# All five late token tiles summed by scaled and transposed rows, one tile after the other; gathered v rows turned by half blocks everywhere

## The chip, the cores and the metric

The kernel runs on one core of one Trainium2 chip. The metric is the device time of one execution in microseconds (us). Engines are named as the profile names them: PE (TensorE, the matrix unit), DVE (VectorE), ACT (ScalarE), POOL (GpSimd, here only the issuer of gathers) and SP (SyncE, the issuer of all other transfers).

## What is computed

2048 tokens of width 576 pass through two branches and a gate:

```python
g = sigmoid((x * gate_w).sum(-1, keepdims=True))
a = irfft2(rfft2(x) * (w_r + 1j * w_i))            # spectral branch
q = einsum("nd,dhc->nhc", x, w_q)                  # 32 heads, two halves of 128
s1, s2 = q[..., :128] @ k1.T, q[..., 128:] @ k2.T  # 64 scores each
i1, i2 = argmax(s1), argmax(s2)                    # one expert of 4096 per token and head
e = i1 * 64 + i2
gain = softmax(best s1 + best s2)                  # over one candidate
act = gelu(einsum("nd,nhd->nh", x, u[e]))
b = einsum("nh,nh,nhd->nd", gain, act, v[e])       # expert branch
out = g * a + (1 - g) * b
```

## The kernel before

**Tiles and chunks.** The tokens are 16 tiles of 128; the 32 heads are 8 chunks of 4. For each of the 64 pairs of (chunk, two tiles) PE multiplies x by a folded query matrix (`mh`, `ml`, x split into `xh`, `xo`, `xq`, so that products are exact enough for an argmax), DVE takes the maxima (L577), ACT and DVE turn them into expert numbers (L584 to L633). For each tile, chunk and head POOL then issues one indirect transfer (L671) that brings 128 rows of 4608 bytes, u and v of the chosen experts side by side, into a buffer `uv`. There are 512 such gathers. 12 buffers hold them, 15 from the second half on; the matrices for the next chunk (`uv<-wqT`) use the same 12.

**What is done with a gathered group of four rows** (function `group`): DVE takes the four dot products of u and x (L683), ACT the gelu (L689), DVE multiplies by the gain (L698; L693 in the very last group, head by head). Then the v rows are summed over the heads in one of two ways, which `how(t, c)` picks:
- "v": DVE multiplies each v row by its factor and adds it to an accumulator (L709 for the first, L711 for the others). The buffer is free after that.
- "t": ACT scales each v row (L724); scaled rows of two heads stand side by side in one buffer, and PE transposes this pair block by block into PSUM, where the heads are added. The buffers are free after that. An early tile adds each chunk's PSUM to `yt` on DVE (L771) and is turned back at the end (L1115); a late one stays in PSUM over its chunks and is turned back by PE at its end, with two ACT copies (L754, L758).

PE's transposes come in two forms (`turn`): whole blocks (9 matmuls of 128x128 for a pair), or half blocks, 64 rows each on half of the array (18 matmuls of 64 columns for a pair). `HALF` is for early tiles and `HALF_L` for late ones. `TJ` and `TJ_L` say after how many rows PE is called.

**Stages.** Tiles 0 to 10 are "early": their gathers run while PE works on the scores. Tiles 11 to 15 are "late": their gathers come after all early ones, in the order of `SEQ`, while PE, ACT and DVE work on the spectral branch: a first stage on x (`fold`; tiles in `FOLD_V` add and subtract the halves of x on DVE first, L889 and L891, and need fewer matmuls), the middle (`f2`, `f4`, `f5`, `f6`, L917 to L1057), and the inverse (`invert`; tiles not in `INV_P` do two DVE steps, L1094 and L1095, in place of half of the last matmuls). `mix` (L1115, L1118) puts both branches together, and SP writes the tile.

**The order** of each engine's instructions is written out ahead by a planner (`Plan.order`): it runs through the jobs with assumed durations, priorities (`at`) and pools, and each engine then works strictly in the order found. Numbers such as `LEAD`, `TPS`, `TLAG`, `XN0` or `BUILD` are its assumptions and priorities: they move instructions and change none. All engines' instructions of a kind come from one line (all PE work is L372), so the profile tells them apart by tiles.

The lines around which the change turns, before:

```python
if mode == "v":
    ...
        dv(0.731, at, lambda v=v, s=s: stt(y.ap, v(), s(), y.ap, op0=ALU.mult, op1=ALU.add), [y], [(rows[k], 1), (a, k)])
    return
last = c == NCH - 1 - (TAILV if t == SEQ[-2][0] and t in T_T else 0)
...
half = HALF_L if t >= NE else HALF
for k in range(HPC):
    if mode == "t":
        ...
        ac(0.667, at + AT_SCALE, ...)          # L724
        tj = TJ_L if t >= NE else TJ
        if k % tj < tj - 1:
            continue                           # PE is called after tj rows
```

Of the kernel before, what the change touches and what calls it, by code (L numbers as in the profile page):

```python
# [27 lines left out]
NCH = 8  # L28
# [60 lines left out]

LAG = {"DVE": 0.1, "ACT": 0.2, "PE": 0.0}  # L90
HOPS = {('PE', 'DVE'): 0.12, ('PE', 'ACT'): 0.46, ('PE', 'POOL'): 0.64, ('ACT', 'PE'): 0.28, ('ACT', 'DVE'): 0.02, ('ACT', 'POOL'): 0.01, ('DVE', 'POOL'): 0.4}
LEAD = 1.341
LEAST = -11.809
LAND = 4.039
ALONE = 0.716
SHARE = 0.426
WINDOW = 3.41
DENSE = -2.439
SLOWER = 1.649


class Plan:
# [37 lines left out]
    def order(self):  # L140
# [77 lines left out]
        while events:  # L218
            t = events[0][0]
            while events and events[0][0] <= t:  # L220
# [26 lines left out]
            for eng, q in todo.items():  # L247
# [60 lines left out]
def tile_kernel(ctx, tc, xn, xT, wqT, wqL, kT, wri, uv, uw, gw, t_kr, t_fi, t_fe, t_tw, t_io, out):  # L308
# [151 lines left out]
    last = {}  # L460
# [200 lines left out]
    def group(t, c, at, ahead, gate_by=()):  # L661
# [49 lines left out]
                    dv(0.731, at, lambda v=v, s=s: stt(y.ap, v(), s(), y.ap, op0=ALU.mult, op1=ALU.add), [y], [(rows[k], 1), (a, k)])  # L711
            return
        part = t in E_T
        last = c == NCH - 1 - (TAILV if t == SEQ[-2][0] and t in T_T else 0)
        part_ = part and not paired(t, c)
        first = c == 0 or (part and not paired(t, c - 1))
        if first:
# [459 lines left out]
TPS = 7.047
AHEAD = -45.811
TLAG = 27.448
FPACE = 1.413  # L1180
# [26 lines left out]
ISSUE = 0.845
MOVE = 1.368
X_GAP = 4.311
GATE = -10.202  # L1210
HOLD_ML = 1.992
HOLD_A = 0.08
HOLD_T = 0.263
# [5 lines left out]
AT_GELU = -46.223
AT_SCALE = 9.213  # L1220
AT_SUM = -94.03
AT_FOLD = -9.381
# [11 lines left out]
TP0 = 12.235
X2 = 59.927
X4 = -0.154
XN0 = 11.008
INV_P = (0, 1, 2, 4, 8, 9, 10, 12, 14, 15)
SOLO = 0
SOLO_AT = -7.687  # L1240
SGO0 = 22.859
SOLO_P = 222.219
GL0 = 208.398
GL = 1.201
# [66 lines left out]
```

## Time and profile before

| | |
|---|---|
| median of 3 runs | 948.02 us (943.16 to 948.95) |
| profiled execution, its own time | 941.52 us |
| its span, first to last instruction | 939.7 us, 18504 instructions |
| mean granted PE clock | 0.972 |
| busy: PE, DVE, ACT, POOL | 866.9, 815.9, 641.3, 559.1 us |
| transfers | 344.16 MB, of which 302.02 MB are gathers |

A row of the windows view gives, for a stretch of the span, the busy time of each engine with its number of instructions, the granted PE clock (1.00 is full), the mean busy share of the 16 DMA engines, and GB/s. Shares just over 1 come from packets that overlap. A row of the groups gives line, engine, operation, tiles, shapes and count, then the busy time in us and the mean duration of one in ns, then the engine's idle time just ahead of it and what ended that. A row of the timeline gives start, duration, engine, line and operation, and in brackets the idle time ahead and its releaser.

### The profile page before, as it was taken

Reading aid. Unit: us, or ns where it says so; the run is one execution under the profiler, and the core shown is the slowest. Engines: PE = TensorE matmul, PEld = TensorE weight load, DVE = VectorE, ACT = ScalarE, POOL = GpSimd, SP = SyncE. Lnnn points to the kernel's source line nnn. Section 1 sums busy time; section 2 is a strip of 40 time slices with the busy share of each in tenths; the row PEclk is TensorE's granted clock in tenths of the full one; section 3 lists DMA queues with packets and bytes.
Section 4 is the critical chain, followed back from the end, with each engine's and each line's share of the span. In section 5 each row is a group of like instructions: output and inputs, shape, how many; then the busy total and the mean of one; then the engine's idle time right before and its main releaser. Section 6 shows DMA issues by size and latency. Waiting matters only on the chain. (4 is left out here: it accounts for less than half of the span.)

```text
span 939.7 us, 18504 instructions
## 1 busy us (share of the span) xinstructions
PE 866.9 (92%) x6309; PEld 699.4 (74%) x6309; DVE 815.9 (87%) x2036; ACT 641.3 (68%) x2022; POOL 559.1 (59%) x516
## 2 busy tenths in 40 slices
PE   7899999999999998999999999967989999979993
PEld 6678887887877887888787777755767788756662
DVE  3578998998999999899999989898988898887888
ACT  3779888877877776876877777664646656654443
POOL 0416767756756656665665665667666556667560
PEclk9999999999999999999999999997999999999997
DMA  8968999999999999999999999899999999999993
GB/s 272 380 224 314 386 404 363 397 401 372 365 393 368 384 391 361 360 390 380 362 400 386 383 391 417 317 337 415 328 417 341 367 380 395 415 351 412 379 419 131
DMA packets 93218, 344.16 MB, mean 366 GB/s; under 512 B 10306, under 2 KB 14020, under 8 KB 93124
## 3 DMA queue, kind: packets, MB, share of 16 engines
q0 software_dynamic: 73728, 302.02, 83.7%
q1 hardware_dynamic: 19396, 40.96, 11.9%
q8 instruction: 50, 0.82, 0.3%
q14 instruction: 44, 0.36, 0.1%
HBM read 338.22 MB, written 4.72 MB: 365 GB/s over the span
## 5 line engine op out<-in xcount | busy, mean ns | idle before, releaser
L584 ACT ACTIVATE sg<-p,mx 128x64 bf16<-128x64 f32 x1024 | 227.1, 353 | 86.8 <-DVE mx L577 63.3
L671 POOL DMA_INDIRECT uv<-uv,eq x176 | 189.5, 1077 | 161.8 <-DVE xn L711 48.1
L683 DVE SCALAR_TENSOR_TENSOR uv<-uv,xn 128x576 f32<-128x576 f32 x352 | 259.9, 749 | 13.9 <-DMA uv<-uv,ei 4.6
L671 POOL DMA_INDIRECT uv<-uv,ei x178 | 199.9, 1123 | 104.8 <-issue 32.5
L724 ACT ACTIVATE uv<-uv,a 128x576 f32<-128x576 f32 x316 | 223.3, 784 | 19.7 <-DVE a L698 16.2
L372 PE MATMUL p<-ident,uv 64*128 64x64 f32 (+1 forms) x1980 | 159.7, 249 | 13.8 <-ACT uv L724 9.6
L372 PEld LDWEIGHTS p<-ident,uv 64*128 64x128 f32 (+1 forms) x1980 | 138.7, 140 | 41.3 <-ACT uv L724 16.7
L711 DVE SCALAR_TENSOR_TENSOR xn<-uv,a,xn 128x576 f32<-128x576 f32 x190 | 154.2, 812 | 0.5
L671 POOL DMA_INDIRECT uv<-uw,eq x80 | 88.2, 1103 | 52.5 <-issue 13.6
L683 DVE SCALAR_TENSOR_TENSOR uv<-uv,xl 128x576 f32<-128x576 f32 x160 | 116.0, 751 | 0.2
L372 PE MATMUL p<-mh,xha 128*128 128x512 f32 x256 | 106.3, 415 | 3.6 <-issue 2.4
L671 POOL DMA_INDIRECT uv<-uw,ei x78 | 81.2, 1042 | 41.0 <-issue 15.3
L372 PE MATMUL p<-mh,xh 128*128 128x512 f32 x256 | 103.5, 404 | 0.4 <-ACT sg L584 0.4
L372 PE MATMUL p<-ml,xha 128*128 128x512 f32 x256 | 101.1, 395 | 1.4 <-issue 1.4
L372 PE MATMUL p<-ml,xh 128*128 128x512 f32 x256 | 101.2, 395 | 0.6 <-issue 0.6
L372 PE MATMUL p<-mh,xoa 128*128 128x512 f32 x256 | 101.0, 395 | 0.5 <-issue 0.3
L372 PE MATMUL p<-mh,xo 128*128 128x512 f32 x256 | 101.1, 395 | 0.0
L372 PE MATMUL p<-fi,bt 128*128 128x289 f32 (+1 forms) x384 | 89.9, 429 | 1.1 <-ACT bt L917 0.7
L577 DVE TENSOR_REDUCE mx<-p 128x16 f32<-128x1024 f32 x64 | 77.9, 1218 | 13.9 <-PE p L372 11.8
L372 PEld LDWEIGHTS p<-fi,bt 128*128 128x128 f32 (+1 forms) x384 | 67.6, 242 | 19.1 <-issue 12.1
L606 ACT ACTIVATE sg<-sg 128x256 bf16<-128x256 bf16 x192 | 73.6, 424 | 0.8
L689 ACT ACTIVATE b<-z 128x4 f32<-128x4 f32 (+1 forms) x131 | 29.8, 228 | 62.7 <-DVE uv L683 52.1
(142 smaller groups left out, 1333.4 us busy)
## 6 DMA issues: line engine op xcount, KB each, us to landing
uv<-wqT SPq DMA_DIRECT2D x32, 512.0 KB
w<-wri SPq DMA_DIRECT2D x16, 289.0 KB
ml<-xT SPq DMA_DIRECT2D x16, 256.0 KB
xn<-xn SPq DMA_DIRECT2D x11, 288.0 KB
out<-xn SPq DMA_DIRECT2D x10, 288.0 KB
uv<-uv,ei POOLq DMA_INDIRECT x178
uv<-uv,eq POOLq DMA_INDIRECT x176
uv<-wqL SPq DMA_DIRECT2D x8, 256.0 KB
```

Source lines behind the costliest of these rows:

```text
L372: after("PE", nc.tensor.matmul(*args, **kw))
L577: dv(dve(1024), at - MXO, lambda: nc.vector.tensor_reduce(mv.ap[:, 2 * tp : 2 * tp + 2, :], ps.ap.rearrange("p a (g e) -> p a g e", e=E), ...
L584: on("ACT", actv(sg.ap[:, j, g, :], ps.ap[:, j, g * E : g * E + E], AF.Sign, bias=mv.ap[:, 2 * tp + j, g : g + 1], scale=-1.0))
L606: ac(0.307 if j is None else 0.2, at_, lambda b=b, s2=s2: actv(s2()[:, :, b * Q : b * Q + Q], s2()[:, :, b * Q : b * Q + Q], AF.Copy, bias ...
L671: on("POOL", nc.gpsimd.indirect_dma_start(out=g.ap.rearrange("p a d -> p (a d)"), out_offset=None, in_=table, in_offset=bass.IndirectOffse ...
L683: dv(0.677, at, lambda k=k, g=rows[k]: stt(g.ap[:, 0, :], g.ap[:, 0, :], 1.0, x.ap, op0=ALU.mult, op1=ALU.mult, accum_out=z.ap[:, k : k + 1]),
L689: ac(0.1, at + AT_GELU, lambda k0=k0, k1=k1: actv(b.ap[:, k0:k1], z.ap[:, k0:k1], AF.Gelu_apprx_tanh), [(b, k0)], [(z, k) for k in ks], ta ...
L711: dv(0.731, at, lambda v=v, s=s: stt(y.ap, v(), s(), y.ap, op0=ALU.mult, op1=ALU.add), [y], [(rows[k], 1), (a, k)])
L724: ac(0.667, at + AT_SCALE, lambda k=k, pair=pair, r=r: actv(pair.ap[:, r, :], rows[k].ap[:, 1, :], AF.Copy, scale=a.ap[:, k : k + 1]), [(p ...
```

## The change

- Late tiles. Before, tile 15 was summed the "v" way in all chunks, and tile 11 the "t" way except for its last chunk; the two were interleaved chunk by chunk at the end. Now all five late tiles are "t", one after the other (11, 14, 12, 13, 15), and only the last chunk of the last tile, 15, is "v". PE is called after two rows, not four (`TJ_L`).
- Early tiles. Six of eleven stay "t" (others than before), now with half blocks (`HALF`).
- Spectral branch. 3 tiles in place of 11 fold on DVE first; 7 in place of 10 do the long form of the inverse.
- The first pair of tiles is handled tile by tile (`SOLO`: two maxima of 512, L573, in place of one of 1024), and the planner's numbers differ, so that everything is in a new order.

```diff
-        last = c == NCH - 1 - (TAILV if t == SEQ[-2][0] and t in T_T else 0)
+        last = c == NCH - 1 - tail(t)
...
-LEAD = 1.341
+LEAD = 0.765
...
-BUILD = (3, 5, 6, 7, 7)
+BUILD = (2, 5, 5, 6, 6)
...
-_PAIRS = ((14,), (13,), (12,), (11, 15))
+_PAIRS = ((11,), (14,), (12,), (13,), (15,))
...
-HALF = 0
+HALF = 1
 HALF_L = 1
+TAILW = 1
...
-TJ_L = 4
+TJ_L = 2
...
-T_T = (2, 3, 4, 6, 7, 10, 11, 12, 13, 14)
+T_T = (1, 3, 5, 6, 7, 10, 11, 12, 13, 14, 15)
...
-FOLD_V = (0, 1, 4, 5, 6, 8, 10, 11, 12, 13, 14)
+FOLD_V = (0, 3, 8)
...
-TAILV = 1
+TAILV = 0
...
-INV_P = (0, 1, 2, 4, 8, 9, 10, 12, 14, 15)
-SOLO = 0
+INV_P = (0, 1, 4, 6, 7, 14, 15)
+SOLO = 1
...
+def tail(t):
+    if t not in T_T:
+        return 0
+    return TAILW if t == SEQ[-1][0] else TAILV if t == SEQ[-2][0] else 0
...
 def how(t, c):
-    if t == SEQ[-2][0] and c >= NCH - TAILV:
+    if c >= NCH - tail(t):
         return "v"
```

**Where instructions move.** First, the end of DVE's order. Of the two accumulators before, `xn_11043` is tile 11's and `xn_10218` tile 15's. Before:

```order
L683 SCALAR_TENSOR_TENSOR uv_10922,z_11050<-uv_10922,xl_7143 128x576
L711 SCALAR_TENSOR_TENSOR xn_11043<-uv_10877,a_11048,xn_11043 128x576
L693 SCALAR_TENSOR_TENSOR a_11061<-b_11053,gone,swl_7718 128x1 x2
L711 SCALAR_TENSOR_TENSOR xn_11043<-uv_10899,a_11048,xn_11043 128x576
L693 SCALAR_TENSOR_TENSOR a_11061<-b_11053,gone,swl_7718 128x1
L711 SCALAR_TENSOR_TENSOR xn_10218<-uv_10903,a_11061,xn_10218 128x576
L683 SCALAR_TENSOR_TENSOR uv_10960,z_11050<-uv_10960,xl_7143 128x576
L711 SCALAR_TENSOR_TENSOR xn_10218<-uv_10914,a_11061,xn_10218 128x576
L693 SCALAR_TENSOR_TENSOR a_11061<-b_11053,gone,swl_7718 128x1
L1118 SCALAR_TENSOR_TENSOR xn_11043<-xn_11043,gone,xl_10858 128x576
L711 SCALAR_TENSOR_TENSOR xn_10218<-uv_10922,a_11061,xn_10218 128x576
L711 SCALAR_TENSOR_TENSOR xn_10218<-uv_10960,a_11061,xn_10218 128x576
```

And now (`xn_12251` is tile 15's sum, turned back; `xn_10516` tile 13's):

```order
L683 SCALAR_TENSOR_TENSOR uv_11985,z_12174<-uv_11985,xl_7713 128x576
L693 SCALAR_TENSOR_TENSOR a_12187<-b_12184,gone,swl_8513 128x1 x2
L683 SCALAR_TENSOR_TENSOR uv_12011,z_12174<-uv_12011,xl_7713 128x576
L1118 SCALAR_TENSOR_TENSOR xn_10516<-xn_10516,gone,xl_12210 128x576
L693 SCALAR_TENSOR_TENSOR a_12187<-b_12184,gone,swl_8513 128x1
L683 SCALAR_TENSOR_TENSOR uv_12034,z_12174<-uv_12034,xl_7713 128x576
L693 SCALAR_TENSOR_TENSOR a_12187<-b_12184,gone,swl_8513 128x1
L1118 SCALAR_TENSOR_TENSOR xn_12251<-xn_12251,gone,xl_12214 128x576
L711 SCALAR_TENSOR_TENSOR xn_12251<-uv_11954,a_12187,xn_12251 128x576
L711 SCALAR_TENSOR_TENSOR xn_12251<-uv_11985,a_12187,xn_12251 128x576
L711 SCALAR_TENSOR_TENSOR xn_12251<-uv_12011,a_12187,xn_12251 128x576
L711 SCALAR_TENSOR_TENSOR xn_12251<-uv_12034,a_12187,xn_12251 128x576
```

Before, the sums of two tiles alternate at the end; now only the four of tile 15 are left, and they stand behind the mixing of what PE has turned back.

Second, the end of PE's order (`ident,uv` are transposes of gathered pairs, `fi,bt` and `t,krb` the inverse, `ident,f` the turning back). Before:

```order
L372 MATMUL p_1430_10927<-fi_7148,bt_7496 128x289 x6
L372 MATMUL p_1434_10949<-fi_7148,bt_7496 128x289 x6
L372 MATMUL p_1432_10970<-t_1431_10958,krb_7157 128x289 x4
L372 MATMUL p_1625_10180<-ident,uv_10694 128x64 x18
L372 MATMUL p_1625_10180<-ident,uv_10752 128x64 x18
L372 MATMUL p_1436_11021<-t_1435_10975,krb_7157 128x289 x4
L372 MATMUL p_1712_11032<-ident,f_1711_11027 128x128 x4
L372 MATMUL p_1712_11032<-ident,f_1711_11027 128x64 x2
```

And now:

```order
L372 MATMUL p_1419_12110<-fi_7717,bt_8170 128x289 x6
L372 MATMUL p_1670_11720<-ident,uv_11809 128x64 x18
L372 MATMUL p_1417_12146<-t_1416_12122,krb_7747 128x289 x4
L372 MATMUL p_1670_11720<-ident,uv_11856 128x64 x18
L372 MATMUL p_1421_12177<-t_1420_12144,krb_7747 128x289 x4
L372 MATMUL p_1670_11720<-ident,uv_11879 128x64 x18
L372 MATMUL p_1670_11720<-ident,uv_11945 128x64 x18
L372 MATMUL p_1714_12241<-ident,f_1713_12237 128x128 x4
L372 MATMUL p_1714_12241<-ident,f_1713_12237 128x64 x2
```

More transposes stand among the last matmuls of the inverse, and they come one pair at a time.

Third, the start of SP's order (`ml<-xT` is one tile of x for the scores, `mh<-xT` the remainder of four tiles, `xn<-xn` a tile of x for the dot products, `uv<-wqT` a query matrix). Before:

```order
L482 DMA xn_123<-xn 128x576
L482 DMA xn_125<-xn 128x576
L473 DMA ml_129<-xT 128x512
L473 DMA ml_135<-xT 128x512
L482 DMA xn_139<-xn 128x576
L482 DMA xn_150<-xn 128x576
L473 DMA ml_259<-xT 128x512
L469 DMA mh_266<-xT 128x4x128
```

And now:

```order
L473 DMA ml_123<-xT 128x512
L473 DMA ml_125<-xT 128x512
L482 DMA xn_129<-xn 128x576
L482 DMA xn_135<-xn 128x576
L482 DMA xn_139<-xn 128x576
L482 DMA xn_150<-xn 128x576
L428 DMA uv_159<-wqT 128x1024
L473 DMA ml_270<-xT 128x512
L469 DMA mh_274<-xT 128x4x128
```

Tiles 2 and 3 of x moved ahead of the xn rows, and a query matrix of the second chunk (`uv_159`) moved up ahead of the fifth tile.

More of the change, by code (lines that the diff above doesn't have):

```diff
@@ L91 @@
 HOPS = {('PE', 'DVE'): 0.12, ('PE', 'ACT'): 0.46, ('PE', 'POOL'): 0.64, ('ACT', 'PE'): 0.28, ('ACT', 'DVE'): 0.02, ('ACT', 'POOL'): 0.01, ('DVE', 'POOL'): 0.4}
-LEAD = 1.341
[L93 to L96, printed above, removed]
+LEAD = 0.765
+LEAST = -22.748
+LAND = 3.319
+ALONE = 0.665
+SHARE = 0.3
 WINDOW = 3.41
-DENSE = -2.439
-SLOWER = 1.649
+DENSE = -4.803
+SLOWER = 1.318
 class Plan:
@@ L1172 @@
 NG2 = 3
-LE = 3.125
+LE = 2.546
 NE = 11
@@ L1176 @@
 MBL = 8
[L1177 to L1180, printed above, removed]
-BUILD = (3, 5, 6, 7, 7)
+TPS = 7.683
+AHEAD = -0.265
+TLAG = 87.855
+FPACE = 1.962
+BUILD = (2, 5, 5, 6, 6)
 E_T = tuple(range(NE))
 L_SEQ = tuple(range(NE, NT))
-_PAIRS = ((14,), (13,), (12,), (11, 15))
+_PAIRS = ((11,), (14,), (12,), (13,), (15,))
 SEQ = [(t, c) for p in _PAIRS for c in range(NCH) for t in p]
-TGS = 8.225
+TGS = 6.941
 LOW_PE = True
@@ L1202 @@
 Z0 = 0.5
-X0 = 9.48
+X0 = 3.595
 TJ = 2
-TJ_L = 4
+TJ_L = 2
 BUILT = 0.1
[L1207 to L1213, printed above, removed]
+ISSUE = 0.72
+MOVE = 1.331
+X_GAP = 3.48
+GATE = 5.584
+HOLD_ML = 1.701
+HOLD_A = 0.381
+HOLD_T = 0.246
 HOLD_D = 0.0
 D_T = ()
-T_T = (2, 3, 4, 6, 7, 10, 11, 12, 13, 14)
+T_T = (1, 3, 5, 6, 7, 10, 11, 12, 13, 14, 15)
 D_L = ()
 FLIP = ()
[L1219 to L1222, printed above, removed]
-FOLD_V = (0, 1, 4, 5, 6, 8, 10, 11, 12, 13, 14)
-GATE0 = 34.612
+AT_GELU = -16.56
+AT_SCALE = 35.423
+AT_SUM = 9.965
+AT_FOLD = 11.678
+FOLD_V = (0, 3, 8)
+GATE0 = -60.289
 NA = 8
-XL0 = -187.592
-FI0 = -71.365
+XL0 = -76.304
+FI0 = 52.906
 TURN = 1
-MXO = 15.524
-SGO = -56.575
+MXO = 17.514
+SGO = -47.053
 FILL = 0
 FILLED = 8.11
-TAILV = 1
[L1234 to L1237, printed above, removed]
-INV_P = (0, 1, 2, 4, 8, 9, 10, 12, 14, 15)
-SOLO = 0
[L1240 to L1244, printed above, removed]
+TAILV = 0
+TP0 = 3.835
+X2 = 56.51
+X4 = -2.044
+XN0 = 87.616
+INV_P = (0, 1, 4, 6, 7, 14, 15)
+SOLO = 1
+SOLO_AT = 30.626
+SGO0 = -8.738
+SOLO_P = 167.658
+GL0 = 219.19
+GL = 5.575
 TWO = ()
@@ L1248 @@
 SRN = 4
-ODD = (2, 7)
+ODD = (1, 7)
 def paired(t, c):
     return t in TWO and c >= 0 and c + 1 < NCH and c % 2 == (t in ODD)
+def tail(t):
+    if t not in T_T:
+        return 0
+    return TAILW if t == SEQ[-1][0] else TAILV if t == SEQ[-2][0] else 0
 def how(t, c):
-    if t == SEQ[-2][0] and c >= NCH - TAILV:
+    if c >= NCH - tail(t):
         return "v"
```

## Prediction

> **What bounds the kernel now.** I began with the share that each DMA queue takes of the 16 engines' time, then cut the span into stretches, and read the end of the timeline last.
>
> ```profile
> span 939.7 us, 18504 instructions
> q0 software_dynamic: 73728, 302.02, 83.7%
> q1 hardware_dynamic: 19396, 40.96, 11.9%
> q8 instruction: 50, 0.82, 0.3%
> q14 instruction: 44, 0.36, 0.1%
> ```
>
> The queues add up to 96.0%, that is 902 us of 939.7. The change moves no byte: 512 gathers and the same SP transfers remain. So 902 us is a floor as long as packets take what they take here, and at most 38 us can be won. The stretches tell where these 38 us lie:
>
> ```profile
> 0.00:20.00 20.00, 14.60 (x183) 11.98 (x184) 7.10 (x14) 7.45 (x15) 0.20 (x4) 1.00 0.78 269
> 20.00:55.00 35.00, 31.30 (x148) 24.06 (x147) 19.36 (x46) 24.05 (x100) 10.53 (x11) 0.90 1.00 375
> 55.00:80.00 25.00, 24.60 (x216) 19.74 (x215) 22.02 (x53) 21.31 (x77) 7.97 (x7) 1.00 0.58 169
> 80.00:590.00 510.00, 491.51 (x3288) 406.04 (x3287) 466.59 (x1163) 399.44 (x1400) 331.23 (x303) 0.99 1.00 383
> 590.00:630.00 40.00, 35.58 (x254) 29.39 (x252) 34.57 (x91) 27.28 (x93) 23.70 (x22) 0.96 0.88 311
> 630.00:920.00 290.00, 263.75 (x2174) 203.90 (x2173) 249.73 (x637) 157.45 (x330) 185.50 (x172) 0.96 0.99 385
> 860.00:925.00 65.00, 64.97 (x453) 46.23 (x452) 53.59 (x122) 29.97 (x64) 35.37 (x33) 1.00 0.98 384
> 923.30:939.70 16.40, 2.23 (x14) 1.75 (x12) 13.23 (x29) 2.34 (x8) 0.00 (x0) 0.66 0.14 54
> ```
>
> From 80 to 590 the DMA share (next to last number) is 1.00: the stream of gathers sets the pace there, though PE with 491.5 of 510 us is close behind. The idle DMA time is 4.4 us up to 20, 25 x 0.42 = 10.5 us from 55 to 80, 40 x 0.12 = 4.8 us from 590 to 630, 2.9 us from 630 to 920, and some 14 us after the stream, from about 923.3 on. And the row from 860 to 925 shows PE full (64.97 of 65) beside a DMA that is nearly full: at the end two engines run level, and the chain that ended last indeed runs back through PE's inverse. What follows the stream is DVE's:
>
> ```profile
> 918.46 0.93 POOL L671 DMA_INDIRECT uv<-uv,ei  x1 [3.48 <-ACT t L1083]
> 934.18 0.81 DVE L1118 SCALAR_TENSOR_TENSOR xn<-xn,gone,xl 128x576 f32<-128x576 f32 x1
> 934.91 1.66 DVE L711 SCALAR_TENSOR_TENSOR xn<-uv,a,xn 128x576 f32<-128x576 f32 x2
> 936.60 0.33 SPq L1145 DMA_DIRECT2D out<-xn  x1
> ```
>
> The last gather is issued at 918.46, the stream falls silent near 923.3, DVE's last sum ends at 936.57, and the write takes until 939.7: a tail of 16.4 us, 13.2 of them full of DVE work.
>
> **The work that changes engines.** The groups give the durations:
>
> ```profile
> L711 DVE SCALAR_TENSOR_TENSOR xn<-uv,a,xn 128x576 f32<-128x576 f32 x190 | 154.2, 812 | 0.5
> L724 ACT ACTIVATE uv<-uv,a 128x576 f32<-128x576 f32 x316 | 223.3, 784 | 19.7 <-DVE a L698 16.2 <-issue 1.6 <-DMA uv<-uw,ei 1.2
> L372 PE MATMUL p<-ident,uv 128*128 128x128 f32 x864 | 115.3, 278 | 9.6 <-ACT uv L724 9.4
> L372 PE MATMUL p<-ident,uv 64*128 64x64 f32 x1116 | 44.5, 226 | 4.2 <-issue 3.7 <-ACT uv L724 0.2
> L372 PE MATMUL p<-kr,f 128*128 128x128 f32 (+1 forms) x132 | 19.9, 329 | 10.9 <-DVE f L891 10.9
> L372 PE MATMUL p<-kr,xn 128*128 128x128 f32 (+2 forms) x96 | 11.4, 283 | 1.3 <-issue 1.2
> L372 PE MATMUL p<-t,krb 128*128 128x289 f32 x104 | 28.8, 419 | 1.1 <-issue 0.6 <-ACT t L1083 0.4
> L372 PE MATMUL p<-ident,f 128*128 128x128 f32 (+1 forms) x32 | 4.1, 272 | 1.6 <-ACT f L754 1.1 <-issue 0.5
> L889 DVE TENSOR_TENSOR f<-xn 128x288 f32<-128x288 f32 x7 | 3.1, 450 | 0.8 <-issue 0.8
> L1094 DVE TENSOR_TENSOR t<-p,t 128x289 f32<-128x289 f32 x6 | 2.7, 454 | 1.6 <-ACT t L1093 1.6
> ```
>
> DVE: 32 v sums fewer at 0.81 us, -26 us; 8 folds less with two steps of 0.45, -7.2; three more short inverses with two steps of 0.454, +2.7. Together about -30 us, all in the late part. ACT: 32 scalings more at 0.784, +25 us, also late, where it is busy 157 of 290 us: that is covered by its idle time, and if the cover went (a scaling that stands behind another engine's work) each would delay its own pair only.
>
> PE, early: 96 pairs go from 115.3/96 = 1.20 us to 44.5/62 = 0.72, -46 us. I count this as nothing in the sum, since the DMA share is 1.00 over these 510 us and PE was not the bound; it widens PE's margin there. PE, late: 16 more pairs at 0.72, +11.5; eight folds at 11.4/4 = 2.85 in place of 19.9/11 = 1.81, +8.3; one turning back, 4.1/4, +1.0; three inverses with four matmul instructions fewer at 28.8/104 = 0.28, -3.3. Together +17.5 us. In 590 to 920 PE has 4.4 + 26.2 = 30.7 us free, and 10.9 of PE's waits were for the fold steps on DVE that now go. So the cover is there on the whole, but not from 860 on, where PE has none. In the built order, after the transposes of gather 464 (of 512) PE has left: before 10 pairs of transposes, and of the inverses' last step 13, seven of them long; now 22 pairs and 12 last steps, five of them long (12 matmul instructions fewer); one late turning back more, one early one less. That is 12 x 0.72 - 12 x 0.28 = +5.3 us. That price is real if PE is still late when it gets there.
>
> **The tail, new.** Behind the last landing stands what the last chunk but one needs, whose rows land some four gathers earlier. A gather costs 83.7% x 939.7/512 = 1.54 us, so 6.1 us earlier. From there, with these rows
>
> ```profile
> L683 DVE SCALAR_TENSOR_TENSOR uv<-uv,xl 128x576 f32<-128x576 f32 x160 | 116.0, 751 | 0.2
> L689 ACT ACTIVATE b<-z 128x4 f32<-128x4 f32 (+1 forms) x131 | 29.8, 228 | 62.7 <-DVE uv L683 52.1
> L754 ACT ACTIVATE f<-p 128x640 f32<-128x640 f32 x4 | 2.8, 700 | 1.7 <-PE p L372 1.7
> L758 ACT ACTIVATE xn<-p 128x576 f32<-128x576 f32 x4 | 2.6, 644 | 0.0
> L698 DVE SCALAR_TENSOR_TENSOR a<-b,swl 128x4 f32<-128x4 f32 x31 | 4.9, 159 | 10.5 <-ACT b L689 5.8 <-issue 3.4 <-ACT tw L959 1.1
> 861.36 1.28 PE L372 MATMUL p<-ident,uv 64*128 64x64 f32 x36
> ```
>
> a dot 0.75, gelu 0.23, factor 0.16, four scalings 3.1, two pairs 1.28, the ACT copy 0.70, the turning back 1.0, the second copy 0.64, the mixing 0.81 and four sums 3.2 make 11.9 us, with some 2 us for eight hand-overs (an estimate from the 0.2 to 0.5 us between the pieces at the end of the chain) 13.9. Less 6.1 that is 7.8 after the last landing, and with the write of 3.1 us (936.57 to 939.7) 10.9. Against 16.4 this is **-5.5 us**. Bounds: nothing is won if PE or ACT is late there (0); if the turned-back sum is ready in time, only a dot, a gelu, a factor, one sum, hand-overs and the write remain, about 5.5 us, which is -11.
>
> **The start.** The ring of buffers runs full after 11 gathers, and POOL waits:
>
> ```profile
> 47.03 0.94 POOL L671 DMA_INDIRECT uv<-uw,eq  x1 [2.15 <-remote]
> 65.97 0.93 POOL L671 DMA_INDIRECT uv<-uv,eq  x1 [18.00 <-DVE xn L711]
> 41.04 0.39 PE L372 MATMUL p<-mh,xha 128*128 128x512 f32 x1 [0.95 <-issue]
> 60.33 1.28 ACT L689 ACT_TABLE_LOAD   x1
> 62.45 0.51 DVE L709 TENSOR_SCALAR xn<-uv,a 128x576 f32<-128x576 f32 x1
> ```
>
> The first buffer is freed by L709, behind ACT's table load and gelu, which stand in ACT's order behind three quarters of the fifth pair of tiles' signs (L584). Now they stand behind a quarter, and the gathers begin after one tile; on the other hand one building of a query matrix stands ahead of the third pair on PE (51.6 us for 40 of them in its group, so 1.3 us). PE's gaps around 41 to 46 us, which the row puts to nothing but issue, fall in a time of full DMA that remains. I take **-3 us**: of the bounds +2 (the building delays all, nothing is won) and -10.5 (all idle time from 55 to 80 goes) it is nearer to the first, since the full ring and the chain that frees it stay.
>
> **The end of the scores.** From 590 to 630 the gathers wait for scores and for full engines. PE's last score now stands behind transposes up to gather 294, not 306, and each is shorter, so the last expert numbers come earlier against the stream. I take **-3 us**, between 0 and -4.8.
>
> **Sum:** -5.5 - 3 - 3 = -11.5, so the profiled time of 941.5 us would become 930. The runs shown have their median 6.5 us above the profiled execution; I move the difference over and get 948.0 - 11.5, rounded **936.5 us**.
>
> **A rule that speaks against it.** The trace has one form of late call, 36 half-block matmuls at once, two pairs, in 1.28 us. The Trainium skill (TensorEngine Tiling (Array Packing), Key Properties) says that a change of the tiling mode drains PE, and calls with one pair, among full-width matmuls, change it twice as often. The row shows that two switches and 36 matmuls fit into 1.28 us; no row shows a call of 18. By the rule a lone pair costs more than half of it, 0.64; if it came to the 0.90 of a whole-block pair (an estimate, from 585.22 to 586.12 in the rows below), the 92 pairs from the first fold on would add 24 us to PE, and the last rival would grow by as much.
>
> ```profile
> 585.22 1.14 PE L372 MATMUL p<-ident,uv 128*128 128x128 f32 x9
> 586.12 0.48 PE L372 MATMUL p<-mh,xh 128*128 128x512 f32 x1
> ```
>
> **Rivals.**
> - *PE sets the end, and no more than a little is won.* PE is full from 860 to 925, and gets 5.3 us more there. It ended near 925.5 (2.23 us of work after 923.3) and would end at 930.8; copy, mixing, sums, hand-overs and the write (0.64 + 0.81 + 3.2 + 0.5 + 3.1) add 8.3, which is 939.1 against 939.7: -1 us, **947 us**. For it: the full row. Against it: late pairs no longer wait for four rows, and PE gets to its late work with less behind it. 37%.
> - *PE is late from the first fold on.* The first fold starts where it did (just before 598) and PE has as much idle time as before in the late part, because its waits come from others; then all 17.5 us come on top: 925.5 + 17.5 + 8.3 = 951.3 against 939.7, +12, **960 us**. It decides the sign as soon as over 6 of the 17.5 us find no gap. Against it: the gaps of 30.7 us, and the fold waits that go. 13%.
> - *The order is moved and the stream's idle time only changes its place* is part of the first rival: the tail alone gives 942.5.
>
> **How the numbers follow.** A measurement here tells about 1% (9.5 us) from no change. Forecast, 50%: from 922 (all three gains at their bounds: -26) to 942. The first rival, 37%: 938.5 to 951. The last one, 13%: above. Range 922 to 951, which leaves out the last rival. Faster by over 1% means under 938.5: most of the forecast's part and some of its neighbour, 0.50; within 1%: 0.37; slower: 0.13.
>
> **What would show it.** Right: DMA share 1.00 from 80 to 590 as before, under 10 us idle from 55 to 80, a DVE tail with four L711 behind one L1118, the last sum some 8 us after the stream falls silent, half-block pairs at about 0.72 us in all parts. Wrong: a PE that is full for more than the last 65 us, a DMA share under 0.97 in the late part, or a stall at the start as long as before.

## The result, and the profile after

The changed kernel takes **957.71 us** (median of 4 runs, 957.34 to 966.65) against 948.49 (median of 4) for the kernel before, timed beside it: ratio 1.0113, 95% interval 1.0067 to 1.0159. All ratios and intervals here leave out single runs in a slow state. I had forecast 936.5 with a range of 922 to 951; the time lies outside it, on the other side of the kernel before.

The head of the page, and the windows view with the cuts of the prediction (the last row is again the stretch behind the last gathered packet):

```profile
span 955.8 us, 21053 instructions
q0 software_dynamic: 73728, 302.02, 83.3%
q1 hardware_dynamic: 19396, 40.96, 11.5%
```

```profile
0.00:20.00 20.00, 14.09 (x184) 11.30 (x185) 7.01 (x14) 7.60 (x15) 0.20 (x4) 1.00 0.87 300
20.00:55.00 35.00, 32.03 (x189) 25.49 (x187) 23.97 (x62) 28.23 (x112) 10.32 (x10) 0.97 0.97 351
55.00:80.00 25.00, 24.21 (x212) 19.11 (x211) 20.24 (x52) 20.53 (x73) 11.95 (x12) 0.97 0.73 249
80.00:590.00 510.00, 471.35 (x3919) 364.03 (x3918) 440.88 (x1101) 385.56 (x1329) 311.62 (x286) 0.99 0.97 365
590.00:630.00 40.00, 37.88 (x246) 30.98 (x247) 34.85 (x91) 31.13 (x129) 21.85 (x20) 0.93 0.87 321
630.00:920.00 290.00, 271.58 (x2556) 212.47 (x2556) 237.20 (x630) 174.71 (x358) 192.61 (x179) 0.97 1.00 390
860.00:925.00 65.00, 64.03 (x611) 47.54 (x610) 40.16 (x109) 42.72 (x82) 41.93 (x40) 1.00 0.99 386
937.70:955.80 18.10, 9.16 (x103) 6.79 (x101) 10.16 (x22) 7.73 (x18) 0.00 (x0) 0.86 0.14 52
```

From 80 to 590 the DMA share fell from 1.00 to 0.97 and the rate from 383 to 365 GB/s, while PE and DVE also do less per us than before. Nothing is full there any more. Late, the share rose from 0.99 to 1.00. The gathers' packets took 83.3% of 955.8, 796 us, against 786.5 before, for the same packets and bytes.

Where the time went is clearest from the gathers' issue times (each from its row of POOL's timeline, counted from 0):

| us | before | after | difference |
|---|---|---|---|
| start to gather 44 | 121.1 | 124.3 | +3.2 |
| gather 44 to 308 | 451.0 | 472.9 | **+21.9** |
| 308 to 352 (last scores) | 75.8 | 73.4 | -2.4 |
| 352 to 511 | 270.6 | 259.4 | -11.2 |
| 511 to the end | 21.2 | 25.9 | +4.7 |
| span | 939.7 | 955.8 | +16.1 |

The medians are only 9.2 us apart, as the profiled execution of before, 941.52, lies 7.0 us under this median; the picture is the same in a second pair of profiles below. From 100 us to gather 308, the rows of POOL's timeline with 3.5 us and more of idle time (in brackets) are these eleven; before, there was a single one (at 134.97, 4.17 us):

```profile
124.27 0.94 POOL L671 DMA_INDIRECT uv<-uv,eq  x1 [4.67 <-ACT sg L606]
201.95 0.95 POOL L671 DMA_INDIRECT uv<-uv,eq  x1 [4.98 <-ACT sg L606]
230.66 0.94 POOL L671 DMA_INDIRECT uv<-uv,eq  x1 [3.54 <-ACT uv L724]
278.59 1.30 POOL L671 DMA_INDIRECT uv<-uw,ei  x1 [5.00 <-DVE fe L626]
354.43 1.21 POOL L671 DMA_INDIRECT uv<-uv,ei  x1 [5.85 <-DVE xn L711]
426.56 1.21 POOL L671 DMA_INDIRECT uv<-uv,ei  x1 [3.60 <-ACT uv L724]
466.54 0.94 POOL L671 DMA_INDIRECT uv<-uv,eq  x1 [4.50 <-ACT uv L724]
494.81 1.16 POOL L671 DMA_INDIRECT uv<-uv,ei  x1 [4.29 <-issue]
544.30 1.04 POOL L671 DMA_INDIRECT uv<-uv,eq  x1 [3.74 <-DVE uv L683]
582.56 1.37 POOL L671 DMA_INDIRECT uv<-uv,ei  x1 [4.56 <-PE p L372]
597.18 1.06 POOL L671 DMA_INDIRECT uv<-uv,eq  x1 [5.86 <-ACT eq L633]
```

The releasers differ, and the one in brackets is only the last that the profile can name. At 201.95 and 597.18 (gathers 88 and 308, each the first of a chunk of 44) the expert number comes late; at most others a buffer comes free late, by DVE's sums, ACT's scalings or PE's transposes.

At the end, the chain of work that ended last (from 915 us on) runs through PE before it comes to DVE's sums:

```profile
914.96 30.87 PE p L372 x288
...
945.85 0.71 ACT f L754
...
946.61 1.06 PE p L372 x8
...
947.69 0.66 ACT xn L758
...
948.38 0.83 DVE xn L1118
```

PE is busy without a break until 945.8, eight us after the last packet (937.7), and the copies, the mixing and four sums come behind it: 18.1 us of tail against 16.4.

### The profile page after: what moved, and what is told of

It is laid out like the page before. It is cut to its first block, busy times and chain, and to the rows that moved or that the text cites. A ratio compares the mean times of both kernels' runs of the same rounds, so it can differ in the third digit from the quotient of the medians.

```text
span 955.8 us, 21053 instructions
## 1 busy us (share of the span) xinstructions
PE 878.0 (92%) x7553; PEld 683.5 (72%) x7553; DVE 787.0 (82%) x2001; ACT 667.9 (70%) x2052; POOL 555.4 (58%) x516
## 3 DMA queue, kind: packets, MB, share of 16 engines
q0 software_dynamic: 73728, 302.02, 83.3%
## 4 chain that ended last, share of the span: by engine, by line
PE 38%; DVE 23%; DMA 10%; ACT 9%; issue 8%; POOL 6%; another core or an unknown queue 3%; POOLq 0%; ACTq 0%; DVEq 0%
PE p L372 38%; DVE uv L683 9%; DMA uv<-uv,eq 6%; POOL uv L671 6%; DVE xn L711 4%; ACT sg L584 3%; ACT uv L724 3%; DVE mx L577 2%; DMA uv<-uw,eq 2%; DMA uv<-uv,ei 2%; DVE yt L771 2%; DVE uv L489 1%; ACT sg L606 1%; DVE t L984 1%
## 5 line engine op out<-in xcount | busy, mean ns | idle before, releaser
L671 POOL DMA_INDIRECT uv<-uv,eq x176 | 191.5, 1088 | 153.3 <-issue 33.2
L724 ACT ACTIVATE uv<-uv,a 128x576 f32<-128x576 f32 x348 | 248.0, 774 | 34.7 <-DVE a L698 19.3
L671 POOL DMA_INDIRECT uv<-uv,ei x162 | 172.7, 1066 | 109.8 <-PE p L372 30.7
L372 PEld LDWEIGHTS p<-ident,uv 64*128 64x128 f32 x3132 | 115.1, 139 | 69.9 <-issue 40.5
L372 PE MATMUL p<-ident,uv 64*128 64x64 f32 x3132 | 138.2, 229 | 20.1 <-issue 11.3
L671 POOL DMA_INDIRECT uv<-uw,ei x94 | 102.4, 1089 | 62.3 <-issue 16.3
L711 DVE SCALAR_TENSOR_TENSOR xn<-uv,a,xn 128x576 f32<-128x576 f32 x159 | 129.2, 813 | 0.2
L372 PE MATMUL p<-mh,xh 128*128 128x512 f32 x256 | 107.5, 420 | 16.3 <-DVE yt L771 14.2
L372 PE MATMUL p<-fi,bt 128*128 128x289 f32 (+1 forms) x384 | 92.2, 434 | 2.0 <-DVE bt L1057 0.7
L606 ACT ACTIVATE sg<-sg 128x256 bf16<-128x256 bf16 (+1 forms) x195 | 75.1, 436 | 0.9
```

The source lines that it names most:

```text
L372: after("PE", nc.tensor.matmul(*args, **kw))
L606: ac(0.307 if j is None else 0.2, at_, lambda b=b, s2=s2: actv(s2()[:, :, b * Q : b * Q + Q], s2()[:, :, b * Q : b * Q + Q], AF.Copy, bias ...
L671: on("POOL", nc.gpsimd.indirect_dma_start(out=g.ap.rearrange("p a d -> p (a d)"), out_offset=None, in_=table, in_offset=bass.IndirectOffse ...
L724: ac(0.667, at + AT_SCALE, lambda k=k, pair=pair, r=r: actv(pair.ap[:, r, :], rows[k].ap[:, 1, :], AF.Copy, scale=a.ap[:, k : k + 1]), [(p ...
```

## The experiments

The runs came in five groups, each on one chip, with the kernel before timed beside them; ratios are to that. The chips differ: the kernel before took 960.0 us in the first group, 893.6, 948.1, 892.7 and 893.7 in the others. Stage times are compared within a group, or between groups of the same speed. My first theory was that experts' numbers stand too late in the new order (A), the rival that the half blocks of early tiles do the harm (B).

**e1: one number of the plan put back.**

```diff
-LE = 2.546
+LE = 3.125
```

> The changed kernel with one number of its plan put back, LE (the time that the plan allows from a score to the expert number) from 2.546 to 3.125 us. Half blocks and the five late tiles stay. In VectorE's order the first gather of a chunk now has 8 to 13 row dots ahead of its expert number's step, where the changed kernel has 5 to 8 and the kernel before 8 to 9. Theory A (the order: gathers run dry at the chunk starts since their numbers stand too late): the stretch from the issue of gather 44 to that of gather 308 falls from 472.9 us to about 451, the median from 957.7 to 935 to 942, DMA share 80 to 590 back to 1.00. Theory B (the half blocks of the early tiles hold TensorE and so the scores): the stretch stays at 468 to 475 and the median within 4 us of 957.7.

997.62 us, ratio 1.0415 (1.0321 to 1.051), the stretch 44 to 308 at 494.6 us. Both theories miss it, and A in the form I gave it falls: the expert numbers now stand on DVE further ahead of the gathers' own dots (7 to 13 dots ahead at the chunk starts, 5 to 8 in the changed kernel), and the time got longer. It shows how much the order alone can do: one number of the plan, the same work, and a ratio 3% over that of the changed kernel.

**e2, e3: the form of early transposes, at a fixed order.**

```diff
         half = HALF_L if t >= NE else HALF
+        cost = half
+        half = half if t >= NE else 0      # e2; in e3: half = 1
...
-                plan("PE", 9 * len(pairs) * TRANS2 + SWITCH if half else ...
+                plan("PE", 9 * len(pairs) * TRANS2 + SWITCH if cost else ...
```

> The changed kernel in its own order, but the early tiles' transposes issued as whole blocks again (the plan still counts them as half blocks, so that no engine's order moves). Theory A (order): stretch 44 to 308 stays at 468 to 475 us, median 953 to 962. Theory B (half blocks): stretch about 451, median 935 to 942. If both share it, half of it: 460 to 464, median about 946.

> The kernel before in its own order, with the early tiles' transposes issued as half blocks and nothing else changed. Theory A (order): nothing, 451 us from gather 44 to 308, median 944 to 952, since TensorE's busy time falls by some 8 us and its idle time grows by about as much. Theory B (half blocks): the whole loss, stretch about 470, median 966 to 972. My own sum of the prediction (46 us off TensorE, off the path): nothing either, with TensorE's busy time 80 to 590 down by 46.

e2: 960.25 us, 1.0017 (0.9979 to 1.0055), but its stretch 44 to 308 is still 470.2. e3: 967.66 us, 1.0097 (1.0059 to 1.0136). B seems to hold in the total and fails in the place: without half blocks the middle stays long. Beside the totals of this group stands a rival that no run tests: the mean granted clock was 0.983 in e2, 0.959 in e3 and 0.965 in the kernel before.

**e4: the late part of the change alone.**

```diff
-_PAIRS = ((14,), (13,), (12,), (11, 15))
+_PAIRS = ((11,), (14,), (12,), (13,), (15,))
-TJ_L = 4
+TJ_L = 2
-T_T = (2, 3, 4, 6, 7, 10, 11, 12, 13, 14)
+T_T = (2, 3, 4, 6, 7, 10, 11, 12, 13, 14, 15)
-TAILV = 1
+TAILV = 0
+TAILW = 1
```

> The kernel before with the late part of the change alone: five late tiles one at a time, all five summed on TensorE but for the last chunk; early tiles, their whole blocks and every number of the plan as before. If the late part alone carries what the changed kernel won behind gather 308 (346.4 to 332.7 us), the stretch 44 to 308 is 451 and the late one 331 to 336: median 933 to 939. If that gain came from the early part's lag (the queue behind it fuller or emptier at 308) or from the new order, the late stretch stays at 343 to 348: median 945 to 951.

965.2 us, 1.0067 (1.0029 to 1.0105): a loss, not the gain of 13.7 us. The stretch 308 to 511 is 342.9 us, and behind the last packet come 25.4 us; the chain that ended last has PE without a break to 948.5:

```profile
914.78 33.68 PE p L372 x265
```

**e5 to e8: the change taken apart on one chip.** e5 is the kernel before and e6 the changed one, once more; e7 is the new order alone (e2's edit, and late tiles as before; it keeps the changed kernel's set of early tiles and its `FOLD_V`, `INV_P` and `SOLO`, of which e15 and e17 below try all but the last), e8 the same with half blocks:

```diff
-_PAIRS = ((11,), (14,), (12,), (13,), (15,))
+_PAIRS = ((14,), (13,), (12,), (11, 15))
-TJ_L = 2
+TJ_L = 4
-T_T = (1, 3, 5, 6, 7, 10, 11, 12, 13, 14, 15)
+T_T = (1, 3, 5, 6, 7, 10, 11, 12, 13, 14)
-TAILV = 0
+TAILV = 1
```

> The kernel before, unchanged, for its stages on the chip that the other runs of this group use: the one profile of it is from another run, and its times in the first group lay 12 us above that one's (960.0 against 948.5). If that is the rate of the whole machine, each stage is 1.2% longer (gather 44 to 308 456 us, 308 to 511 350, tail 16.6). If it falls on the rows' stream alone, the stretches that the stream fills grow and the start and tail stay.

> The changed kernel, unchanged, beside e2 on one chip's footing. If the half blocks of the early tiles carry the loss (e2 without them stood at 1.0017 of the kernel before, e3 with them alone at 1.0097), it stands 0.8 to 1.1% over the kernel before, most of it between gathers 44 and 352. If the first measurement's 1.0113 was chance, it lies within 0.4% of the kernel before.

> The new order alone: every number of the changed kernel's plan, but whole blocks for the early tiles and the late tiles as before (the last two together, the last chunk of one by VectorE). Sum theory (half blocks +1.0%, late tiles +0.7%, order -0.5%, worked out from e2, e3 and e4): ratio 0.990 to 0.998. Order theory (the new order costs 22 us between gathers 44 and 308, and the late tiles win it back): ratio 1.010 to 1.025, the stretch 44 to 308 at 470 and the late stretch 345 to 352.

> The new order and the half blocks of the early tiles, the late tiles as before. Sum theory: 1.002 to 1.008, that is 1.0% over e7 and 0.7% under the changed kernel. Order theory: 1.015 to 1.03.

| | median | ratio | 0 to 44 | 44 to 308 | 308 to 352 | 352 to 511 | to the end | PE busy |
|---|---|---|---|---|---|---|---|---|
| e5 before | 892.26 | 0.9989 | 112.4 | 431.0 | 71.9 | 254.9 | 21.9 | 843.8 |
| e7 order alone | 901.48 | 1.0085 (1.0064 to 1.0106) | 121.0 | 438.8 | 66.7 | 250.2 | 22.1 | 846.4 |
| e8 and half blocks | 900.91 | 1.0087 (1.0063 to 1.0111) | 119.5 | 439.5 | 67.4 | 249.3 | 22.3 | 840.6 |
| e6 and late tiles | 902.70 | 1.0107 (1.0082 to 1.0131) | 119.8 | 437.3 | 66.4 | 248.4 | 26.6 | 853.2 |

The new order alone is most of the loss. Half blocks take 5.8 us off PE and change the time by nothing here; the late tiles add 12.6 us to PE and 0.2%, within the intervals. Neither theory has both sizes: e7 lies far from the sum theory (0.990 to 0.998) and just under the order theory (1.010 to 1.025), but e8 misses both ranges and lies nearer to the sum theory's (up to 1.008, against 1.015 and more). Adding up e2 to e4 fails, since half blocks cost 1% in the old order (e3) and nothing in the new one; and the late tiles don't win the loss back, since e7 makes it up without them.

The order loses 16.4 us up to gather 308 (8.6 at the start, 7.8 in the middle) and makes 9.9 up behind it. The same stretch, from the start to gather 308, in e5 and in e7:

```profile
0.00:543.37 543.37, 530.79 (x3746) 440.85 (x3747) 496.05 (x1233) 436.31 (x1528) 341.58 (x313) 1.00 0.99 386
0.00:559.79 559.79, 540.65 (x3788) 448.71 (x3789) 498.69 (x1245) 447.12 (x1554) 331.89 (x312) 1.00 0.98 381
```

PE is busy 9.9 us longer in e7, with 42 matmuls more, all of them scores of three further pairs of tile and chunk (3 x 14), and idle 6.6 us longer. So 9.9 of the 16.4 us are score work that the new order puts ahead of gather 308 and the old one behind it, as much as is made up later; what is lost for good is the idle time. The waits of the gathers show the order too: 3.5 us and more, from 100 us to gather 308, at two places in e5 and at nine in e7, seven of which (gathers 44, 88, 130, 173, 252, 302 and 308) are among the eleven of the changed kernel.

**e9 to e12: an engine relieved, the order kept.** e9 (on before) and e10 (on after) leave out score matmuls; e11 and e12 do DVE's sums in early tiles on 64 of 576 columns, so that most of these sums is left out:

```diff
                 for n, (xx, m) in enumerate(seq):
+                    if n == 1 and i < 2:
+                        continue
```

```diff
-... stt(y.ap, v(), s(), y.ap, op0=ALU.mult, op1=ALU.add)
+w = E if t < NE else D
+... stt(y.ap[:, :w], v()[:, :w], s(), y.ap[:, :w], op0=ALU.mult, op1=ALU.add)
```

> The kernel before, in its order, with 256 score matmuls left out (in blocks 0 and 1 of each half score, the product of x with the low part of m); the scores are then a little coarser. At 0.23 us each that takes 58 us off TensorE before gather 352, somewhat more than the 46 us that the prediction took off the early tiles and counted at nothing. Stream theory (my prediction: from 80 to 590 us the rows' stream sets the pace): the stretch from gather 44 to 308 as long as in the kernel before, ratio 0.995 to 1.000. TensorE theory (TensorE is the bound, and the stream goes at full share because its packets get longer while rows stand in the 12 buffers): the stretch 20 to 45 us shorter, ratio 0.95 to 0.98.

> The changed kernel with the same 256 score matmuls left out. Stream theory: ratio 1.005 to 1.011, as without it. TensorE theory: as far under the changed kernel as e9 is under the kernel before, ratio 0.96 to 0.99. Order theory (the new order makes engines wait for each other, whatever TensorE has to do): under 1.011, but by less than half of e9's gain.

> The kernel before, in its order, with the 155 sums of v rows on VectorE in early tiles (line 711, 0.81 us each) done on 64 of 576 columns. That takes about 100 us off VectorE before gather 352, and the rows' buffers come free sooner. Stream theory: stretch 44 to 308 unchanged, ratio 0.995 to 1.000. TensorE theory: nearly nothing, 0.99 to 1.00. Buffer theory (12 row buffers, each held some 17 us from issue to release, set the pace: 17.4 us by 10.2 buffers is 1.71 us a gather): each v row is held about 1.5 to 3 us less, the stretch 25 to 50 us shorter, ratio 0.95 to 0.975.

> The changed kernel with the same cut of VectorE's sums in early tiles. Stream theory: 1.005 to 1.011. TensorE theory: 1.00 to 1.01. Buffer theory: the stretch 44 to 308 falls to that of e11, ratio 0.955 to 0.985.

| | ratio | engine time off, ahead of gather 352 | 44 to 308 |
|---|---|---|---|
| e9 before, less PE | 0.9927 (0.9886 to 0.9967) | PE 46.6 us | 446.3 (451.0) |
| e11 before, less DVE | 0.9816 (0.9752 to 0.9879) | DVE 72.9 | 440.3 (451.0) |
| e10 after, less PE | 1.0006 (0.9973 to 1.0039) | PE 38.3 | 465.3 (472.9) |
| e12 after, less DVE | 1.0050 (1.0008 to 1.0092) | DVE 73.1 | 467.4 (472.9) |

The chip was as fast as that of the first measurement, whose stretch stands in brackets. The row 80 to 590 of e9, e11, e10 and e12:

```profile
80.00:590.00 510.00, 457.39 (x3067) 370.59 (x3066) 469.89 (x1169) 401.34 (x1418) 329.55 (x300) 0.97 1.00 385
80.00:590.00 510.00, 497.09 (x3336) 412.42 (x3335) 410.22 (x1186) 406.11 (x1430) 321.68 (x306) 1.00 1.00 389
80.00:590.00 510.00, 448.65 (x3737) 340.98 (x3737) 447.46 (x1125) 392.47 (x1370) 313.32 (x289) 0.95 0.97 369
80.00:590.00 510.00, 476.68 (x3933) 370.36 (x3932) 385.25 (x1115) 389.42 (x1360) 296.31 (x287) 0.97 0.98 370
```

Two readings. In the first two rows the DMA share is 1.00 as in the kernel before, and yet the bytes go faster, 385 and 389 GB/s in place of 383: a share of 1.00 was no floor. And none of the theories has the size right: PE's relief gives 7 us in the old order (46.6 us off) and 10 in the new one (38.3 off); 73 us off DVE give 17 in the old order and 6 in the new one. The order theory had e10 gain less than half of what e9 gains, and it gained no less: with PE relieved, the new order is level with the unrelieved old one in total. PE's relief was also smaller than the 58 us that I reckoned; the granted clock in these rows is 0.97 and 0.95 in e9 and e10, against 0.99 in the two kernels with all matmuls, which may be a part of that. Yet in the stretch 44 to 308 the new order stays at a DMA share of 0.97 to 0.98 with either relief, and over 14 us behind even the unrelieved old one, while PE is busy only 448.7 of 510 us in e10 and DVE 385.3 of 510 in e12. So its loss there isn't the load of PE alone or of DVE alone; that engines wait for each other fits, but no run isolates it.

**e13 to e16: how deep the stream runs.** A buffer comes free when its row has been used; in the fixed orders of DVE, ACT and PE, other rows' work stands ahead of that use, and these rows must have landed. I call the depth of a gather its number less that of the last such row: the gathers that can be under way while it waits. One number changed each (two in e16):

```diff
-T_T = (1, 3, 5, 6, 7, 10, 11, 12, 13, 14, 15)      # e13 and e16, on after
+T_T = (2, 3, 4, 6, 7, 10, 11, 12, 13, 14, 15)
-AT_SCALE = 35.423                                  # e16 alone
+AT_SCALE = 9.213
-HALF = 1                                           # e14, on after
+HALF = 0
-T_T = (2, 3, 4, 6, 7, 10, 11, 12, 13, 14)          # e15, on before
+T_T = (1, 3, 5, 6, 7, 10, 11, 12, 13, 14)
```

> The changed kernel with the early tiles that are summed on TensorE as in the kernel before (2, 3, 4, 6, 7, 10 in place of 1, 3, 5, 6, 7, 10), nothing else. Its plan comes out with deeper flight: of the gathers 44 to 308 none has a depth of 4 or less, 2 have 5 and 12 have 6 (changed kernel: 4, 2, 14; before: 0, 10, 11; e1, which was 4.15% slower: 5, 6, 22). Depth theory: the stretch 44 to 308 near that of the kernel before, and with the late part's gain a ratio of 0.990 to 1.002. If the tile set and the depths don't matter: 1.008 to 1.014.

> The changed kernel with HALF = 0: whole blocks for the early tiles, this time in the plan too, so that the order is another one than e2's. Depths of 4 or less: 12 gathers, three of them at each chunk's start with 3. Depth theory: each of these waits some 2 to 4 us, ratio 1.03 to 1.06, well over e2 (1.0017), though the same work is done in the same form. If depths don't matter: as e2, 0.998 to 1.006.

> The kernel before with the changed kernel's early tiles on TensorE (1, 3, 5, 6, 7, 10). Depths: none at 4 or less, 4 at 5, 26 at 6. Depth theory: within 0.5% of the kernel before. If the tile set itself is what costs (say, that tile 1 is summed on TensorE), it shows here as 1.008 or more.

> As e13, and AT_SCALE (where ScalarE's scaling of a row stands in the plan) as in the kernel before, 9.213 in place of 35.423. Depths: none at 4 or less, 1 at 5, 9 at 6, the deepest order of all that were worked out. Depth theory: as e13 or up to 0.5% under it, 0.985 to 1.000, and if anything beats the kernel before, this does.

e14 came, in its total, as the depth theory has it: 926.49 us, 1.0384 (1.0336 to 1.0432). Between 100 us and gather 308, POOL waits 3.5 us or more at seven places and these alone: gathers 44, 88, 132, 176, 220, 264 and 308, the chunk starts:

```profile
121.88 1.03 POOL L671 DMA_INDIRECT uv<-uv,eq  x1 [6.46 <-ACT eq L633]
197.25 1.08 POOL L671 DMA_INDIRECT uv<-uv,eq  x1 [7.64 <-ACT sg L606]
271.95 0.94 POOL L671 DMA_INDIRECT uv<-uv,eq  x1 [7.49 <-ACT sg L584]
346.92 0.94 POOL L671 DMA_INDIRECT uv<-uv,eq  x1 [6.30 <-ACT sg L606]
421.95 1.06 POOL L671 DMA_INDIRECT uv<-uv,eq  x1 [7.95 <-ACT mh L526]
497.50 0.94 POOL L671 DMA_INDIRECT uv<-uv,eq  x1 [8.80 <-issue]
574.55 0.94 POOL L671 DMA_INDIRECT uv<-uv,eq  x1 [9.99 <-ACT b L689]
```

At the first six the depth is 4 or 3: on DVE the step that the gather needs (the number's at 44, the sum that frees a buffer at the others) stands behind the dots of rows 40, 85, 129, 173, 217 and 261. The releasers in brackets are not these steps: 88 was let go by a sum (L711) that ended at 196.49. At 308 I find only the number's step, behind the dot of row 302, a depth of 6, on a DVE that was busy without a break from 565.9 on. The waits are 6 to 10 us, not the 2 to 4 of the forecast, and part of e14's loss stands elsewhere: behind gather 511 come 35.1 us, against 25.7 in e2. The same work in the same form, in another order, is 1.0017 in e2 and 1.0384 here (e2 on another chip; the intervals are far apart). But e13, with hardly a shallow place, is 1.0112 (1.0044 to 1.018), and e16 1.0128 (1.0081 to 1.0175): as the changed kernel. Their stretch 44 to 308 is 436.7 and 435.3 us, still 4 to 6 over e5's 431.0, and the start is as long (122.0 and 122.2 to gather 44). So shallow places cost where there are any, but they aren't what the changed kernel lost. e15 is 1.0015 (0.9991 to 1.0039): the other set of early tiles costs nothing by itself.

**e17, e18: the late numbers, with the early order of before.**

```diff
-FOLD_V = (0, 1, 4, 5, 6, 8, 10, 11, 12, 13, 14)
+FOLD_V = (0, 3, 8)
-INV_P = (0, 1, 2, 4, 8, 9, 10, 12, 14, 15)
+INV_P = (0, 1, 4, 6, 7, 14, 15)
```

with AT_FOLD, FPACE, TLAG, TGS, XL0, FI0, GL0 and GL of the changed kernel; e18 has e4's edit as well.

> The kernel before with only those numbers of the new order that place late work (which tiles' inverse is made on TensorE and which folds VectorE sums, INV_P and FOLD_V; and the times of fold, late rows, late loads and late gates, AT_FOLD, FPACE, TLAG, TGS, XL0, FI0, GL0, GL). The order of all engines up to about gather 340 is word for word that of the kernel before; late tiles and whole blocks as before. Two separate things (late numbers win, early ones lose): behind gather 308 it is 8 to 14 us shorter (from e7 against e5: 5.2, 4.7 and 3.7 us), nothing is lost ahead of it, ratio 0.985 to 0.992, the fastest of all. One thing (the late gain is the early loss made up): ratio 0.997 to 1.003.

> As e17, and the five late tiles one at a time, all summed on TensorE but for the last chunk, as in the changed kernel. From e4 (1.0067) and from e6 against e8 (0.2%) the late tiles cost 0.2 to 0.7%: ratio 0.987 to 0.999 if e17 is at 0.985 to 0.992, with TensorE some 14 us busier behind gather 352 and VectorE 20 us less. If the late tiles in truth win and only stood in a bad order in e4: under e17 by 0.3% or more, as the prediction's 5.5 us of the tail would have it.

e17: 894.16 us, 0.9996 (0.9972 to 1.002). e18: 894.35 us, 1.0012 (0.9984 to 1.004). The late gain of the new order doesn't come along: from 308 to 511 e17 needs 325.0 us against e5's 326.8, e7 316.9. So that gain does not belong to the late numbers; it is the early loss made up, as far as it is the 9.9 us of score work that e7 does ahead of gather 308. e18's PE is busy 861.3 of 890.2 us, 17.5 more than e5's, at no cost that shows. No version was measured faster than the kernel before at its full work.

## Why the prediction was wrong

**The step that failed** is the reading of the middle: "the stream of gathers sets the pace there", and so that a new order of DVE, ACT and PE costs nothing between 80 and 590 us. I priced the order at the start (-3), at the scores' end (-3) and in the tail (-5.5), and gave the 510 us between nothing in either direction. There the kernel lost 21.9 us, and with the order alone, on a faster chip, 7.8. The sum also had no term for score work that moves ahead of gather 308 (9.9 us in e7). The share of 1.00 told that packets were always under way, not that they could not be faster or be kept waiting: e9 and e11 move them faster at the same share, and with the new order it falls to 0.97. The floor of 902 us had a condition, that packets take what they took, and it doesn't hold: their time was 786.5 us in before, 796 in after, 779 in e11 (83.9% of 929.0), and e5, on a faster chip, ended its span at 892.1.

**Rivals.** None of the three had this mechanism. "PE sets the end" was right in its place: PE was full from 860 to 945.8. Its price, -1 us, was wrong, since PE came 20 us later than the 925.5 from which I reckoned; most of that is the late stream.

**Early PE, -46, counted as nothing.** Both halves were off. I divided summed durations, which overlap, by the number of pairs. The timelines show what a pair takes out of PE's sequence; before (whole blocks) and after (half blocks):

```profile
305.34 0.39 PE L372 MATMUL p<-mh,xoa 128*128 128x512 f32 x1
305.57 1.14 PE L372 MATMUL p<-ident,uv 128*128 128x128 f32 x9
306.47 0.47 PE L372 MATMUL p<-mh,xha 128*128 128x512 f32 x1
306.78 0.39 PE L372 MATMUL p<-ml,xha 128*128 128x512 f32 x1
```

```profile
305.46 0.40 PE L372 MATMUL p<-mh,xo 128*128 128x512 f32 x1
305.79 0.77 PE L372 MATMUL p<-ident,uv 64*128 64x64 f32 x18
306.49 0.50 PE L372 MATMUL p<-mh,xh 128*128 128x512 f32 x1
306.82 0.40 PE L372 MATMUL p<-ml,xh 128*128 128x512 f32 x1
```

From the score matmul ahead to the second one behind it is 1.44 us with whole blocks and 1.36 with half blocks: 0.08 a pair, some 8 us in 96 pairs, and 5.8 by e8 against e7. (The medians of over 60 such calls in each trace are 1.45 and 1.36.) PE's whole busy time rose by 11.1 us where I had -28.5. And PE's time wasn't free either: 46.6 us less of it, in e9, gave 7 us. Score matmuls follow one another at 0.23 us, as does a whole-block call behind one; the half-block call starts 0.33 behind the one ahead of it. Behind the call, the next two score matmuls are 0.33 apart after half blocks and 0.31 after whole ones. The rule of the Trainium skill (TensorEngine Tiling (Array Packing), Key Properties), that a change of the tiling mode drains PE, fits the 0.10 us ahead of the call; the time behind it hardly tells the two forms apart. The lone pair itself takes 0.70, between the 0.64 and the 0.90 that I had set.

**Late PE, +17.5, covered.** Right on the whole: e18 has 17.5 us more PE time than e5 and is no slower, and e6 against e8 12.6 us for 0.2%. Not right at the end, where I saw that cover was missing: see the tail.

**The tail, -5.5.** It became +1.7. I let it start from the rows' landing; it starts from PE, which was still at transposes and inverses for eight us. The pieces behind it (0.71, 1.06, 0.66, 0.83, four sums) came as written. In e4 the same change of tiles made it 9 us longer.

**The start, -3.** Gather 16 came 5.2 us earlier (72.5 in place of 77.7), as meant, but by gather 44 this was lost: +3.2, and +8.6 in e7 against e5. Beyond the usual 0.30 us between two gathers, POOL waits 13.7 us between them, and 1.6 before. Some 7 of the 13.7, at gathers 24, 31, 36 and 40, end 0.27 us behind the end of a scaling (L724), and 4.4, at gather 44, behind DVE's L709.

**The end of the scores, -3.** -2.4 from 308 to 352, near in size, and the scores do come earlier against the gathers. But it is no gain: in e7, where the stretch is 5.2 us shorter than in e5, the work that is missing here stands ahead of gather 308, and in e17, with the old early order, nothing is won (72.0 against 71.9).

**DVE and ACT** were right: L711 fell from 190 to 159 sums, L724 rose from 316 to 348, and neither helped:

```profile
L711 DVE SCALAR_TENSOR_TENSOR xn<-uv,a,xn 128x576 f32<-128x576 f32 x159 | 129.2, 813 | 0.2
L724 ACT ACTIVATE uv<-uv,a 128x576 f32<-128x576 f32 x348 | 248.0, 774 | 34.7 <-DVE a L698 19.3 <-issue 5.1 <-DMA uv<-uw,ei 4.1
```

**What stays open:** which of the early numbers make the new order lose some 16 us up to gather 308. LE and AT_SCALE put back, the tile set and the shallow places are ruled out as the whole of it; the others (landing times, BUILD, the times of maxima and signs, the first pair tile by tile) weren't tried alone. Why half blocks cost 1% in e3 and nothing in e8 is open too; the granted clock, 0.959 in e3 against 0.965 beside it, was not held apart from the form. And e7 was on a faster chip than the first measurement, so that the middle's 21.9 us there are not shown to be the order's alone; e2, on a chip as slow, has 470.2 against 459.8 in e4, which has the old early order.

## What to carry to other kernels

A DMA share of 1.00 says that the stream is never empty, not that it sets the pace: where PE is at 96% and DVE at 91% beside it, and a dozen buffers tie them together, price a new order as a risk, even if it moves no work: the orders tried here cost between nothing (e15, e17) and 4.2% (e1), and none gained. What a small operation costs an engine is read from the starts of its neighbours, not from summed durations that overlap. And a late stage that gets faster right behind an early one that got slower has perhaps only caught up: count what each engine has done by the border between them, and put the late edit alone on the old early order before it is counted as a gain.

## What the runs showed of the hardware

The kernel before, unchanged, took 893 to 960 us on different chips, while the changed one stood at 1.011 of it both times that it was measured (beside 948.5 and beside 893.6 us). DVE's instructions did not differ (L711 took 812 and 813 ns in the two profiles of the kernel before). The gathers did (786.5 and 763.6 us of packets), and PE was busy 866.9 us in the one and 843.8 in the other, at a mean granted clock of 0.972 and 0.985; which of the two makes the difference is not shown. The page of e5 and its row from 80 to 590:

```profile
span 892.1 us, 18504 instructions
q0 software_dynamic: 73728, 302.02, 85.6%
L711 DVE SCALAR_TENSOR_TENSOR xn<-uv,a,xn 128x576 f32<-128x576 f32 x190 | 154.4, 813 | 0.5
80.00:590.00 510.00, 501.77 (x3456) 417.67 (x3455) 484.87 (x1211) 412.78 (x1459) 345.56 (x311) 1.00 1.00 395
```

395 in place of 383 GB/s at the same share of 1.00, the packets' time for the same bytes at 85.6% of 892.1, and PE busy 501.8 of 510 us: there PE has almost nothing left in the middle.
